# A cached-attention decode step on one core: wo in 16-row chunks, head sums replicated over partitions, half of the wo product as quadrant partial sums

## The chip, the cores and the metric

One core of one Trainium2 chip runs the whole program. The metric is the device time of one execution in microseconds (us), the median of several.

## The reference

One decode step for two sequences. A layer norm of `x` feeds two branches: attention over a cache of 32,768 positions (32 query heads over 8 key/value heads of 128), and a small MLP branch whose result gates the attention output.

```python
x  = A_x                                   # [2, 1, 512] bf16
xn = layernorm(x)
q  = (xn @ wq) as 32 heads of 128          # wq [512, 4096]
s  = softmax(q k^T / sqrt(128)) v @ wo     # k, v: [2, 8, 32768, 128]; wo [4096, 512]
g  = silu(B(xn))                           # layernorm, w3, gelu, w4, residual; with one
                                           # position, w1 and w2 meet only zeros
out = x + s * g
```

The bytes decide: K and V are 2 x 134.2 MB, wq 4.2, w3 and w4 3.7, wo 4.2, together 280.5 MB.

## The kernel before

There are 16 groups, one for each sequence and key/value head. For each, K and V (8.4 MB each) stream into SBUF. VectorE (DVE) transposes K, TensorE (PE) forms scores, ScalarE (ACT) takes exponentials, DVE transposes these, and PE multiplies them by V. The sums of group m are finished ("heads") at the start of the next turn of the loop. SyncE (SP) issues all large loads on one queue, each as soon as its buffer is free:

```python
WO_PARTS = [(0, 2, 0, 2048), (2, 4, 0, 2048), (4, 5, 0, 2048), (5, 6, 0, 2048), (6, 7, 0, 2048),
            (7, 8, 0, 1024), (7, 8, 1024, 1536), (7, 8, 1536, 2048)]
# ... wq, w3, w4 and K of group 0 are issued at once
wait(sp, k_h2)                     # the B branch has read w3 and w4, which lie in V's buffer
load_v(0)
for m in range(1, NG):
    sp.wait_ge(p_k, m)             # the first half of K of group m-1 is used up
    load_k(m)
    sp.wait_ge(p_o, m)             # V of group m-1 is used up
    load_v(m)
wos = A_wo.rearrange("(g p r) d -> p g (r d)", p=128, r=NQ)   # NQ = 4: 4 rows of wo = 4 KB
for i, (g0, g1, c0, c1) in enumerate(WO_PARTS):
    d_wo[i].after(sp.dma_start(out=wo3[:, g0:g1, c0:c1], in_=wos[:, g0:g1, c0:c1]), 16)
```

The heads need two rounds between PE and DVE:

```python
def heads(c):                                                  # DVE
    take(dve, s_x)                                             # PE: head_sums
    then(dve.reciprocal(out=rec[:, :], in_=S))                 # [128, 4]
    dve.tensor_mul(out=on[:, :], in0=oT, in1=rec[:, :]).then_inc(s_on, 1)
    take(dve, s_x)                                             # PE: head_rows, 4 matmuls
    then(dve.tensor_mul(out=xm[:, :, :], in0=xp, in1=mask[:, :, :]))
    dve.tensor_reduce(out=oX[:, c], in_=xm[:, :, :], axis=AX.X, op=ALU.add).then_inc(s_r, 1)
# ... PE, at the end: every row of wo times every head row, four column quarters side by side
def product(i):
    # ... wait for piece i, then for each row r of it:
    for n in range(NQ):
        mm = pe.matmul(s_ps[32 * n:32 * n + BW, :], lhsT=oX[:, ...], rhs=wo3[:, g, c:c + QW], ...)
pe.wait_ge(s_r, NG); product(0); head_sums(); product(1); head_rows()
# ... products 2 to 7; those of the last rows wait for the heads of the last group
```

The softmax here doesn't subtract the row's maximum and nothing guards it: scores larger than these inputs give would overflow.

## Time and profile before

| | before |
|---|---|
| time, median of 3 | 655.39 us (655.20 to 655.46) |
| profiled execution | 655.17 us, span 653.8 us |
| moved from HBM | 280.5 MB |
| first data packet begins, last wo packet ends (packet records) | 1.8 us, 650.7 us |

The page gives each engine's busy time and share of the span first, then the DMA queues (packets, megabytes, share of the time of 16 DMA engines).

```profile
PE 403.5 (62%) x2586; PEld 163.9 (25%) x2586; DVE 339.4 (52%) x425; ACT 75.0 (11%) x179; POOL 6.6 (1%) x24
...
q1 hardware_dynamic: 6748, 280.50, 99.3%
```

The windows view gives, for a stretch of time, the busy time of each engine, then the granted PE clock (the share of its full clock that PE was allowed), the DMA share and GB/s:

```profile
60.00:640.00 580.00, 370.25 (x2265) 148.78 (x2262) 307.90 (x365) 63.10 (x152) 0.00 (x0) 0.80 1.00 433
```

No compute engine is near full and the queue is: the span is the DMA stream, plus 1.8 us before it and about 3 us after. The timeline shows how far the engines wait for it. In the middle of the run (columns: start, duration, engine, line, operation; in brackets the idle time before it) it reads:

```profile
299.63 0.33 SPq L208 DMA_DIRECT2D vbuf<-in_A_v_cache_dram  x1
...
303.13 0.17 DVE L508 TENSOR_REDUCE oX<-xm 128x16 f32 x1 [0.24 <-DVEq L46]
312.67 18.14 DVE L488 STREAM_TRANSPOSE T<-kbuf 128x1024 int32<-128x1024 int32 x16 [9.37 <-DVEq L46]
314.06 9.47 PE L552 MATMUL bank<-T,z 128*128 128x512 bf16 x32 [11.49 <-PEq L46]
...
323.69 0.33 SPq L208 DMA_DIRECT2D kbuf<-in_A_k_cache_dram  x1
```

The heads of the last group's sums end at 303.3 us and DVE then waits 9.4 us for the next K. Each later load is issued while earlier ones are still under way, so the queue does not run dry. How long the queue still had work when a load was issued is called that load's lead below. The end is in the chain of waits (start, duration, what; two DVE operations of 0.3 us and the output transfer follow):

```profile
623.93 26.41 DMA kbuf<-in_A_wo_dram
650.35 0.14 issue
650.48 0.53 PE bank L590 x12
651.01 0.01 issue
651.03 0.32 PE bank L590 x4
```

### The profile page before, as it was taken

The numbers are of one execution on the slowest core, as the hardware profiler recorded it, in microseconds if no ns is written. First come the engines' busy times: TensorE is split into PE (matmuls) and PEld (weight loads), VectorE is DVE, ScalarE is ACT, GpSimd is POOL, SyncE is SP. The second block draws the span as 40 slices with busy tenths as digits, with TensorE's granted clock in tenths as the row PEclk, the third lists the DMA queues.
The fourth block names the chain that finished last, engine by engine and source line by source line (L and its number), as shares of the span: only waits on it lengthen the run. The fifth ranks groups of instructions, "written<-read, shape, count | busy, mean of one in ns | idle before, by whom it ended". The sixth has DMA issues, their size and how long they took to land. (4 is left out here: it accounts for less than half of the span.)

```text
span 653.8 us, 6890 instructions
## 1 busy us (share of the span) xinstructions
PE 403.5 (62%) x2586; PEld 163.9 (25%) x2586; DVE 339.4 (52%) x425; ACT 75.0 (11%) x179; POOL 6.6 (1%) x24
## 2 busy tenths in 40 slices
PE   0448295583838658293774829368383946828785
PEld 0123132221313212131231213223131322303332
DVE  3348091653809256290835719174470926538470
ACT  1400102001010200101020010201001020200100
POOL 3000000000000000000000000000000000000000
PEclk9759787786978868698786978778597886959797
DMA  8999999999999999999999999999999999999997
GB/s 368 435 451 445 442 413 433 441 445 429 417 441 445 441 405 449 441 445 405 441 441 445 417 429 441 445 441 405 449 441 445 401 445 441 445 417 423 429 438 296
DMA packets 6765, 280.57 MB, mean 429 GB/s; under 512 B 736, under 2 KB 1000, under 8 KB 2024
## 3 DMA queue, kind: packets, MB, share of 16 engines
q1 hardware_dynamic: 6748, 280.50, 99.3%
q8 instruction: 3, 0.05, 0.0%
q14 instruction: 2, 0.02, 0.0%
q10 hardware_dynamic: 12, 0.01, 0.0%
HBM read 280.50 MB, written 0.00 MB: 429 GB/s over the span
## 5 line engine op out<-in xcount | busy, mean ns | idle before, releaser
L552 PE MATMUL bank<-T,z 128*128 128x512 bf16 x1024 | 282.2, 425 | 163.4 <-PEq L46 158.7
L488 DVE STREAM_TRANSPOSE T<-kbuf 128x1024 int32<-128x1024 int32 x256 | 290.7, 1206 | 124.7 <-DVEq L46 124.7
L552 PEld LDWEIGHTS bank<-T,z 128*128 128x128 bf16 x1024 | 97.8, 103 | 335.0 <-issue 257.4
L570 PE MATMUL bank<-vbuf,pt 128*16 128x512 bf16 x1024 | 74.7, 457 | 1.5 <-PEq L46 1.5
L467 ACT ACTIVATE ep<-bank 128x512 bf16<-128x512 f32 x32 | 19.1, 597 | 439.2 <-ACTq L46 439.2
L503 DVE RECIPROCAL rec<-bank 128x4 f32<-128x4 f32 x17 | 3.1, 182 | 122.2 <-DVEq L46 122.2
L570 PEld LDWEIGHTS bank<-vbuf,pt 128*16 128x16 bf16 x1024 | 28.0, 103 | 40.5 <-issue 23.5
L495 DVE STREAM_TRANSPOSE pt<-ep 128x512 bf16<-128x512 bf16 x32 | 22.1, 690 | 23.4 <-DVEq L46 23.4
L563 PE MATMUL bank<-sm,ones_f 128*128 128x4 f32 x64 | 9.5, 255 | 29.3 <-PEq L46 29.3
L525 PE MATMUL bank<-sel_o,ob 128*128 128x4 f32 x136 | 18.3, 258 | 14.4 <-PEq L46 14.4
L525 PEld LDWEIGHTS bank<-sel_o,ob 128*128 128x128 f32 x136 | 17.3, 199 | 19.0 <-issue 18.9
L471 ACT COPY ob<-bank 128x512 f32<-128x512 f32 x16 | 9.4, 585 | 104.6 <-ACTq L46 104.6
L460 ACT ACT_TABLE_LOAD x16 | 20.5, 1283 | 0.3
L563 PEld LDWEIGHTS bank<-sm,ones_f 128*128 128x128 f32 x64 | 8.6, 195 | 30.2 <-issue 30.2
L533 PE MATMUL bank<-on,sel_r 128*128 128x4 bf16 x68 | 5.6, 165 | 12.8 <-PEq L46 12.6
L460 ACT COPY z<-qr 32x16 bf16 x64 | 12.9, 201 | 0.7
L506 DVE TENSOR_TENSOR xm<-bank,mask 128x16 f32<-128x16 f32 x17 | 3.0, 175 | 11.7 <-DVEq L46 11.7
L295 PE MATMUL bank<-ident,xn_bf 17*128 17x17 bf16 x4 | 0.3, 177 | 13.5 <-POOL x L286 13.5
L520 PE MATMUL bank<-ident 128*1 128x1 bf16 x64 | 8.3, 165 | 0.0
L520 PEld LDWEIGHTS bank<-ident 128*1 128x1 bf16 x64 | 4.0, 81 | 16.1 <-issue 14.2
L533 PEld LDWEIGHTS bank<-on,sel_r 128*128 128x128 bf16 x68 | 3.1, 100 | 13.7 <-issue 13.7
L467 ACT ACTIVATION_READ_ACCUMULATOR ep<-bank 128x1 f32 x32 | 6.4, 199 | 0.2
(71 smaller groups left out, 57.5 us busy)
## 6 DMA issues: line engine op xcount, KB each, us to landing
kbuf<-in_A_k_cache_dram SPq DMA_DIRECT2D x2, 4096.0 KB, 22.8
vbuf<-in_A_v_cache_dram SPq DMA_DIRECT2D x2, 4096.0 KB, 25.6
kbuf<-in_A_wq_dram SPq DMA_DIRECT2D x1, 4096.0 KB, 12.3
vbuf<-in_B_w_dram SPq DMA_DIRECT2D x2, 1792.0 KB, 17.3
kbuf<-in_A_wo_dram SPq DMA_DIRECT2D x2, 1024.0 KB, 33.2
kbuf<-in_A_wo_dram SPq DMA_DIRECT2D x3, 512.0 KB, 35.7
kbuf<-in_A_wo_dram SPq DMA_DIRECT2D x1, 256.0 KB, 26.4
kbuf<-in_A_wo_dram SPq DMA_DIRECT2D x2, 128.0 KB, 15.6
```

Of the source, the lines that this page charges most:

```text
L460: i = act.copy(out=z[32 * j:32 * j + 32, :, :, c:c + rep], in_=qr[32 * j:32 * j + 32, :, :, bass.ds(m * rep, rep)],)
L467: act.activation(out=eps_[i][:, :], in_=sc[i][:, :], func=ACT.Exp, scale=inv_sqrt_dh, accum_out=rss[i][:, :]).then_inc(s_e, 1)
L471: act.copy(out=ob[:, :], in_=o[:, :]).then_inc(s_ob, 1)
L488: dve.transpose(out=Ts[(NR * i + r) % T_BUFS][:, :].rearrange("p (b t k) -> p t b k", b=NB, t=RT), in_=kt[:, r * W:(r + 1) * W].rearrange( ...
L495: dve.transpose(out=pts[h][:, :, :].rearrange("p r (t h) -> p t r h", h=rep), in_=eps_[i][:, :].rearrange("p (t r h) -> p t r h", r=NR, h= ...
L503: then(dve.reciprocal(out=rec[:, :], in_=S))
L520: pe.matmul(mark_ps, lhsT=ident[:, 0:1], rhs=ident[:, 0:1], start=True, stop=True).then_inc(sem, 1)
L525: mm = pe.matmul(oT, lhsT=ob[:, t * Dh:(t + 1) * Dh], rhs=sel_o[:, t, :], start=(t == 0), stop=(t == VT - 1))
L533: mm = pe.matmul(xp[:, r, :], lhsT=sel_r[:, r, :, :].rearrange("p j w -> p (j w)"), rhs=on[:, :], start=True, stop=True,)
L552: mm = pe.matmul(sc[i][:, :], lhsT=z[:, nb, e, zc:zc + 128], rhs=Tb[:, nb, :, e], start=(r == 0 and nb == 0 and e == 0), stop=(r == NR - 1 ...
L563: pe.matmul(S, lhsT=ones_f[:, :], rhs=sms[h][:, :], start=(h == 0), stop=(h == NPART - 1))
L570: mm = pe.matmul(o[32 * j:32 * j + VT * rep, :], lhsT=pts[h][:, r, a * VT * rep:(a + 1) * VT * rep], rhs=vt[:, u * VT:(u + 1) * VT, :].rea ...
```

## The change

The intent: wo is laid out with 16 consecutive rows per partition instead of 4, so that its pieces move in longer runs. The head sums come out replicated over the partitions (by wider selection matrices), and a mask picks each partition's 16 values, which saves the second round between PE and DVE. wo's first half is multiplied early, four rows at a time in the four 32-row quadrants of PE with 512 columns each, and the four partial sums are merged by four fp32 matmuls. Half of group 0's V is issued before the B branch is done, and the B branch's last product no longer uses the quadrants.

```diff
-WO_PARTS = [(0, 2, 0, 2048), (2, 4, 0, 2048), (4, 5, 0, 2048), (5, 6, 0, 2048), ... ]
+WO_PARTS = [(0, 0, 8), (0, 8, 16), (1, 0, 8), (1, 8, 12), (1, 12, 14), (1, 14, 15), (1, 15, 16)]
-    wos = A_wo.rearrange("(g p r) d -> p g (r d)", p=128, r=NQ)
+    wos = A_wo.rearrange("(g p r) d -> p g (r d)", p=128, r=RS)          # RS = 16
 # SP
     load_k(0)
+    load_half(A_v_cache, vbuf[:, :], s_v, 0, 1)
 ...
-    load_v(0)
+    load_half(A_v_cache, vbuf[:, :], s_v, 0, 0)
 # B branch: h2 in one row block, 14 matmuls in turn instead of four side by side
-            h2_ps[32 * j:32 * j + 32, :], lhsT=h_bf[:, f, :], rhs=w4v[:, f, :],
-            start=(f < NQ), stop=(f >= FK - NQ), tile_position=(0, 32 * j),
+        i = pe.matmul(h2[0:32, :], lhsT=h_bf[:, f, :], rhs=w4v[:, f, :], start=(f == 0), stop=(f == FK - 1))
 # heads on DVE
-        then(dve.reciprocal(out=rec[:, :], in_=S))
-        dve.tensor_mul(out=on[:, :], in0=oT, in1=rec[:, :]).then_inc(s_on, 1)
-        take(dve, s_x)
-        then(dve.tensor_mul(out=xm[:, :, :], in0=xp, in1=mask[:, :, :]))
+        then(dve.reciprocal(out=rec[p0:, :], in_=S[p0:, :]))
+        then(dve.scalar_tensor_tensor(out=xm[p0:, :, :], in0=oT ..., scalar=rec[p0:, 0:1], in1=mask ..., mult, mult))
 # PE, the sums: the selection matrix is the stationary side, 128 columns move
-                oT, lhsT=ob[:, t * Dh:(t + 1) * Dh], rhs=sel_o[:, t, :], ...
+                oT, lhsT=sel_o[:, t, :, :, :] ..., rhs=ob[:, t * Dh:(t + 1) * Dh], ...
-    def head_rows(): ...
 # PE, the end
+    def early(i): ...   # row r into e_ps[32 * (r % 4): ...], 512 columns
+    early(0)
     head_sums()
+    k_e = P(early(1))
+    wait(act, k_e)
+    k_es = A(act.copy(out=e_sb[:, :], in_=e_ps[:, :]))
+    pe.wait_ge(s_r, NG + 2)
+    product(2)
+    wait(pe, k_es)
+    for n in range(NQ):  # merge
+        pe.matmul(s_ps[32 * n:32 * n + BW, :], lhsT=sel_w[:, 0:BW], rhs=e_sb[:, n * QW:(n + 1) * QW], ...)
+    for i in range(3, len(WO_PARTS)):
         mm = product(i)
```

(Cut: buffers, masks, their set-up on POOL and DVE, and the copies that gather the heads' rows.)

More of the change, by code (lines that the diff above doesn't have):

```diff
@@ L21 @@
 EPS = 1e-5
-WO_PARTS = [(0, 2, 0, 2048), (2, 4, 0, 2048), (4, 5, 0, 2048), (5, 6, 0, 2048), (6, 7, 0, 2048), (7, 8, 0, 1024), (7, 8, 1024, 1536), (7, 8, 1536, 2048)]
+WO_PARTS = [(0, 0, 8), (0, 8, 16), (1, 0, 8), (1, 8, 12), (1, 12, 14), (1, 14, 15), (1, 15, 16)]
 class Count:
@@ L87 @@
     NQB = Hkv // NQ
+    NS = Hkv // NQ
+    RS = NQ * NQ
+    WL = Dh // RS
     BS = 16
@@ L106 @@
     rss = [sbuf([128, 1], F32, f"rs{i}") for i in range(NPART)]
-    sms = [sbuf([128, rep], F32, f"sm{i}") for i in range(NPART)]
+    sms = [sbuf([128, NQ * rep * WL], F32, f"sm{i}") for i in range(NPART)]
     z = sbuf([128, NB, 2, ZC], BF16, "z")
     ob = sbuf([128, VT * Dh], F32, "ob")
-    rec = sbuf([128, rep], F32, "rec")
-    on = sbuf([128, rep], BF16, "on")
-    xm = sbuf([128, NQ, rep], F32, "xm")
-    oX = sbuf([128, (NG + 1) * NQ], BF16, "oX")
+    rec = sbuf([128, 1], F32, "rec")
+    xm = sbuf([128, WL, RS], F32, "xm")
+    oA = sbuf([128, (NG + 1) * RS], BF16, "oA")
+    oX = sbuf([128, B * NS * RS], BF16, "oX")
     ident = sbuf([128, 128], BF16, "ident")
@@ L116 @@
     sel_w = sbuf([128, 32], F32, "sel_w")
-    sel_o = sbuf([128, VT, rep], F32, "sel_o")
-    sel_h = sbuf([128, rep], F32, "sel_h")
-    sel_r = sbuf([128, NQ, 4, 32], BF16, "sel_r")
-    mask = sbuf([128, NQ, rep], F32, "mask")
+    sel_t = sbuf([128, VT, rep], F32, "sel_t")
+    sel_o = sbuf([128, VT, NQ, rep, WL], F32, "sel_o")
+    sel_u = sbuf([128, rep], F32, "sel_u")
+    sel_h = sbuf([128, NQ, rep, WL], F32, "sel_h")
+    mask = sbuf([128, WL], F32, "mask")
     x_bf = sbuf([128, D], BF16, "x_bf")
-    xf = sbuf([128, D], F32, "xf")
-    xn = sbuf([128, D], F32, "xn")
-    ln2 = sbuf([128, D], F32, "ln2")
+    xf, xn, ln2 = (Ts[0].bitcast(F32)[:, 0:D], Ts[0].bitcast(F32)[:, D:2 * D], Ts[1].bitcast(F32)[:, 0:D])
     xn_bf = sbuf([128, D], BF16, "xn_bf")
@@ L130 @@
     qT = sbuf([128, 32, NQB * 16], F32, "qT")
+    h4 = sbuf([128, QW], F32, "h4")
     qr = sbuf([128, NB, 2, B * Hq], BF16, "qr")
@@ L147 @@
     sc = banks[0:2]
-    o, S_b, oT_b, xp_b, treg_b, s_b = banks[2:8]
-    S = S_b[:, 0:rep]
-    oT = oT_b[:, 0:rep]
-    xp = xp_b[:, 0:NQ * rep].rearrange("p (r h) -> p r h", h=rep)
+    o, S_b, oT_b, h_ps, treg_b, s_b = banks[2:8]
+    S = S_b[:, 0:1]
+    oT = oT_b[:, 0:Dh]
     treg = treg_b[:, 0:2 * DK * 16].bitcast(BF16)
-    h_ps, h2_ps = xp_b, o
+    h2, e_ps = o, sc[0]
+    e_sb = Ts[2].bitcast(F32)[:, 0:D]
     mark_ps = treg_b[0:1, 0:1]
-    h2 = oT_b[:, 0:QW]
     s_ps = s_b[:, 0:QW]
@@ L197 @@
     w34 = vbuf[:, 0:SLOT]
-    wo3 = kbuf[:, 0:Hq * D].rearrange("p (g c) -> p g c", g=Hkv)
+    wo3 = kbuf[:, 0:Hq * D].rearrange("p (g c) -> p g c", g=NS)
     k_w3 = d_w3.after(sp.dma_start(out=w34[:, 0:W4O], in_=B_w3.rearrange("(p k) f -> p (k f)", k=DK)), 16)
@@ L203, with load_half @@
     )
+    def load_half(cache, dst, sems, m, c):
+        w = slice(c * SLOT, (c + 1) * SLOT)
+        sp.dma_start(out=dst[:, w], in_=row_view(cache, *groups[m])[:, w]).then_inc(sems[c], 16)
     def load(cache, dst, sems, m):
-        src = row_view(cache, *groups[m])
         if m < last:
-            sp.dma_start(out=dst, in_=src).then_inc(sems[0], 16)
+            sp.dma_start(out=dst, in_=row_view(cache, *groups[m])).then_inc(sems[0], 16)
             sp.sem_inc(sems[1], 16)
@@ L211, in load @@
             for c in range(NPART):
-                w = slice(c * SLOT, (c + 1) * SLOT)
-                sp.dma_start(out=dst[:, w], in_=src[:, w]).then_inc(sems[c], 16)
+                load_half(cache, dst, sems, m, c)
     def load_k(m):
@@ L246, with wide @@
     k_z0 = G(pool.memset(z[:, :, :, :], 0.0))
+    def wide(t, n):
+        return t.unsqueeze(1).unsqueeze(3).to_broadcast([128, NQ, rep, n])
     V(dve.memset(s_ps, 0.0))
+    V(dve.memset(o[:, :], 0.0))
     V(dve.memset(S, 1.0))
+    V(dve.memset(oX[:, :], 0.0))
     V(dve.memset(h_bf[:, :, :], 0.0))
@@ L299 @@
         dve.tensor_reduce(
-            out=sel_o[:, :, :],
+            out=sel_t[:, :, :],
             in_=ident[:, :].rearrange("p (j a t h) -> p a t h j", j=4, t=VT, h=rep)[:, 0, :, :, :],
@@ L306 @@
         dve.tensor_reduce(
-            out=sel_h[:, :], in_=ident[:, :].rearrange("p (r h) -> p h r", h=rep), axis=AX.X, op=ALU.add
-        )
-    )
-    V(
-        dve.tensor_copy(
-            out=sel_r[:, :, :, :],
-            in_=ident[:, :].rearrange("p (w r) -> p r w", r=NQ).unsqueeze(2).to_broadcast([128, NQ, 4, 32]),
+            out=sel_u[:, :], in_=ident[:, :].rearrange("p (r h) -> p h r", h=rep), axis=AX.X, op=ALU.add
         )
@@ L317 @@
         dve.tensor_reduce(
-            out=mask[:, :, :],
-            in_=ident[:, :].rearrange("p (h w) -> p h w", h=rep).unsqueeze(1).to_broadcast([128, NQ, rep, 32]),
-            axis=AX.X, op=ALU.add,
+            out=mask[:, :], in_=ident[:, :].rearrange("p (j w) -> p w j", w=WL), axis=AX.X, op=ALU.add
         )
@@ L323 @@
     wait(dve, k_w0)
-    k_mask = V(
+    V(
         dve.tensor_reduce(
             out=sel_w[:, 0:BW:BS],
-            in_=ident[:, :].rearrange("p (j r) -> p r j", j=4)[:, 0:B, :], axis=AX.X, op=ALU.add,
+            in_=ident[:, :].rearrange("p (j r) -> p r j", j=4)[:, 0:BW:BS, :], axis=AX.X, op=ALU.add,
         )
@@ L333 @@
     )
+    wait(pool, k_sh, (g_, g_.n))
+    G(pool.tensor_copy(out=sel_h[:, :, :, :], in_=wide(sel_u[:, :], WL)))
+    for t in range(VT):
+        wait(pool, (g_, g_.n))
+        G(pool.tensor_copy(out=sel_o[:, t, :, :, :], in_=wide(sel_t[:, t, :], WL)))
     wq3 = wq_t[:, 0:DK * HD].rearrange("p (k f) -> p k f", k=DK)
@@ L370 @@
     wait(act, k_qT)
-    wait(pool, k_qT)
+    wait(pool, k_qT, (g_, g_.n))
     for n in range(NQ):
@@ L416 @@
     wait(dve, k)
-    k_hb = V(dve.tensor_mul(out=h_bf[:, :, 0:B], in0=hf, in1=th[:, :, :]))
+    k_hb = V(dve.tensor_mul(out=h_bf[:, :, 0:BW:BS], in0=hf, in1=th[:, :, :]))
     wait(pe, k_hb, k_w4)
     for f in range(FK):
-        j = f % NQ
-        i = pe.matmul(
-            h2_ps[32 * j:32 * j + 32, :], lhsT=h_bf[:, f, :], rhs=w4v[:, f, :],
-            start=(f < NQ), stop=(f >= FK - NQ), tile_position=(0, 32 * j),
-        )
+        i = pe.matmul(h2[0:32, :], lhsT=h_bf[:, f, :], rhs=w4v[:, f, :], start=(f == 0), stop=(f == FK - 1))
     k_h2 = P(i)
-    wait(dve, k_h2)
-    k = V(dve.tensor_copy(out=ln2[:, :], in_=h2_ps[:, :]))
-    wait(pe, k, k_mask)
+    wait(act, k_h2)
     for n in range(NQ):
-        i = pe.matmul(
-            h2[32 * n:32 * n + 32, :], lhsT=sel_w[:, :], rhs=ln2[:, n * QW:(n + 1) * QW],
-            start=True, stop=True, tile_position=(0, 32 * n),
-        )
-    k_h4 = P(i)
+        k_h4 = A(act.copy(out=h4[32 * n:32 * n + 32, :], in_=h2[0:32, n * QW:(n + 1) * QW]))
     wait(dve, k_x4, k_h4)
-    k_tf = V(dve.tensor_add(out=t_f[0:QP, :], in0=xn4[0:QP, :], in1=h2[0:QP, :]))
+    k_tf = V(dve.tensor_add(out=t_f[0:QP, :], in0=xn4[0:QP, :], in1=h4[0:QP, :]))
     wait(act, k_tf)
@@ L449 @@
         load_v(m)
-    wos = A_wo.rearrange("(g p r) d -> p g (r d)", p=128, r=NQ)
-    for i, (g0, g1, c0, c1) in enumerate(WO_PARTS):
-        d_wo[i].after(sp.dma_start(out=wo3[:, g0:g1, c0:c1], in_=wos[:, g0:g1, c0:c1]), 16)
+    wos = A_wo.rearrange("(g p r) d -> p g (r d)", p=128, r=RS)
+    for i, (g, r0, r1) in enumerate(WO_PARTS):
+        w = slice(r0 * D, r1 * D)
+        d_wo[i].after(sp.dma_start(out=wo3[:, g, w], in_=wos[:, g, w]), 16)
     wait(act, k_z0, k_qa, k_qg)
@@ L478, in then @@
         take(dve, s_d)
+    sel = sel_h[:, :, :, :].rearrange("p j h w -> p (j h w)")
     def group(odd):
@@ L494, in group @@
             take(dve, s_e)
+            if i == 0:
+                dve.tensor_scalar_mul(out=sms[0][:, :], in0=sel, scalar1=rss[0][:, 0:1]).then_inc(s_d, 1)
             dve.transpose(
@@ L498, in group, with heads @@
             )
-            dve.tensor_scalar_mul(out=sms[h][:, :], in0=sel_h[:, :], scalar1=rss[i][:, 0:1]).then_inc(s_p, 1)
-    def heads(c):
-        take(dve, s_x)
-        then(dve.reciprocal(out=rec[:, :], in_=S))
-        dve.tensor_mul(out=on[:, :], in0=oT, in1=rec[:, :]).then_inc(s_on, 1)
-        take(dve, s_x)
-        then(dve.tensor_mul(out=xm[:, :, :], in0=xp, in1=mask[:, :, :]))
-        with nc.allow_low_precision(reason="three of the four terms are zero, the fourth is bf16"):
-            dve.tensor_reduce(out=oX[:, c], in_=xm[:, :, :], axis=AX.X, op=ALU.add).then_inc(s_r, 1)
+            if i == 1:
+                take(dve, s_d)
+                dve.scalar_tensor_tensor(
+                    out=sms[1][:, :], in0=sel, scalar=rss[1][:, 0:1], in1=sms[0][:, :], op0=ALU.mult, op1=ALU.add
+                ).then_inc(s_p, 1)
+    def heads(dst, p0):
+        take(dve, s_x)
+        then(dve.reciprocal(out=rec[p0:, :], in_=S[p0:, :]))
+        then(
+            dve.scalar_tensor_tensor(
+                out=xm[p0:, :, :], in0=oT[p0:, :].rearrange("p (w r) -> p w r", w=WL), scalar=rec[p0:, 0:1],
+                in1=mask[p0:, :].unsqueeze(2).to_broadcast([128 - p0, WL, RS]), op0=ALU.mult, op1=ALU.mult,
+            )
+        )
+        with nc.allow_low_precision(reason="all terms but one are zero"):
+            dve.tensor_reduce(
+                out=dst, in_=xm[p0:, :, :].rearrange("p w r -> p r w"), axis=AX.X, op=ALU.add
+            ).then_inc(s_r, 1)
     wait(dve, (v_, v_.n))
@@ L513 @@
         for odd in range(2):
-            heads(bass.ds(t * (2 * NQ) + odd * NQ, NQ))
+            heads(oA[:, bass.ds(t * (2 * RS) + odd * RS, RS)], 0)
             group(odd)
-    heads(slice(NG * NQ, (NG + 1) * NQ))
+    oA4 = oA[:, RS:].rearrange("p (b s j r) -> p j (b s) r", b=B, s=NS, j=NQ)
+    oX4 = oX[:, :].rearrange("p (s r) -> p s r", r=RS)
+    for j in range(NQ):
+        n = B * NS if j < NQ - 1 else B * NS - 1
+        w = slice(32 * j, 32 * j + 32)
+        i_c = dve.tensor_copy(out=oX4[w, 0:n, :], in_=oA4[w, j, 0:n, :])
+    i_c.then_inc(s_r, 1)
+    heads(oX4[32 * (NQ - 1):, B * NS - 1, :], 32 * (NQ - 1))
     def mark(sem):
@@ L525, in head_sums @@
             mm = pe.matmul(
-                oT, lhsT=ob[:, t * Dh:(t + 1) * Dh], rhs=sel_o[:, t, :], start=(t == 0), stop=(t == VT - 1)
-            )
-        mm.then_inc(s_x, 1)
-    def head_rows():
-        take(pe, s_on)
-        for r in range(NQ):
-            mm = pe.matmul(
-                xp[:, r, :], lhsT=sel_r[:, r, :, :].rearrange("p j w -> p (j w)"), rhs=on[:, :],
-                start=True, stop=True,
+                oT, lhsT=sel_o[:, t, :, :, :].rearrange("p j h w -> p (j h w)"),
+                rhs=ob[:, t * Dh:(t + 1) * Dh], start=(t == 0), stop=(t == VT - 1),
             )
@@ L541 @@
         head_sums()
-        head_rows()
         take(pe, s_z)
@@ L560 @@
                 mark(p_k)
-        take(pe, s_p, NPART)
-        for h in range(NPART):
-            pe.matmul(S, lhsT=ones_f[:, :], rhs=sms[h][:, :], start=(h == 0), stop=(h == NPART - 1))
+        take(pe, s_p)
+        pe.matmul(S, lhsT=sms[1][:, :], rhs=ones_f[:, 0:1], start=True, stop=True)
         for h in range(NPART):
@@ L578, with o_rows, early @@
         mark(p_o)
-    BO = Hkv * NQ
+    step = NS * RS // BS
+    oXs = oX[:, :].rearrange("p (i s) -> p i s", s=step)
+    def o_rows(g, r):
+        a = g * RS + r
+        return oXs[:, a // step:a // step + BW, a % step]
+    def early(i):
+        g, r0, r1 = WO_PARTS[i]
+        wait(pe, (d_wo[i], 16))
+        for r in range(r0, r1):
+            j = r % NQ
+            mm = pe.matmul(
+                e_ps[32 * j:32 * j + BW, :], lhsT=o_rows(g, r), rhs=wo3[:, g, r * D:(r + 1) * D],
+                start=(r < NQ), stop=(r >= RS - NQ), tile_position=(0, 32 * j),
+            )
+        return mm
     def product(i):
-        g0, g1, c0, c1 = WO_PARTS[i]
+        g, r0, r1 = WO_PARTS[i]
         wait(pe, (d_wo[i], 16))
-        for g in range(g0, g1):
-            for r in range(c0 // D, c1 // D):
-                for n in range(NQ):
-                    c, a = r * D + n * QW, (g + 1) * NQ + r
-                    mm = pe.matmul(
-                        s_ps[32 * n:32 * n + BW, :], lhsT=oX[:, a:a + BO + 1:BO // BS], rhs=wo3[:, g, c:c + QW],
-                        start=(g == 0 and r == 0), stop=(g == Hkv - 1 and r == NQ - 1),
-                        tile_position=(0, 32 * n),
-                    )
-        return mm
-    pe.wait_ge(s_r, NG)
-    product(0)
+        for r in range(r0, r1):
+            for n in range(NQ):
+                c = r * D + n * QW
+                mm = pe.matmul(
+                    s_ps[32 * n:32 * n + BW, :], lhsT=o_rows(g, r), rhs=wo3[:, g, c:c + QW],
+                    start=(r == 0), stop=(r == RS - 1), tile_position=(0, 32 * n),
+                )
+        return mm
+    pe.wait_ge(s_r, NG + 1)
+    early(0)
     head_sums()
-    product(1)
-    head_rows()
-    for i in range(2, len(WO_PARTS)):
-        if WO_PARTS[i][1] == Hkv and WO_PARTS[i - 1][1] < Hkv:
-            pe.wait_ge(s_r, NG + 1)
+    k_e = P(early(1))
[4 more added lines that the diff above has]
+    wait(pe, k_es)
+    for n in range(NQ):
+        pe.matmul(
+            s_ps[32 * n:32 * n + BW, :], lhsT=sel_w[:, 0:BW], rhs=e_sb[:, n * QW:(n + 1) * QW],
+            start=False, stop=False, tile_position=(0, 32 * n),
+        )
+    for i in range(3, len(WO_PARTS)):
         mm = product(i)
```

## The prediction

> **What bounds the kernel now.** The DMA stream. On the page, queue 1 is busy 99.3% of 16 engines' span (653.8 us), moving 280.5 MB; PE is busy 62%, DVE 52%. In the windows view 60 to 640 us runs at 433 GB/s, DMA share 1.00. The trace's packet records agree: a 65,536-byte packet takes 2,418 ns, times 16 engines 433.6 GB/s. The Trainium skill, "DMA: Bandwidth & Descriptors", section "Where 436 GB/s comes from", gives a ceiling of 435.2 GB/s; this trace stands at it. The stream starts about 1.8 us into the span and ends near 650.7; then matmuls, two DVE operations (0.3 us each) and the output transfer follow (chain of waits). Only these two ends, some 5 us, are not streaming, and the bytes do not change.
>
> **The group loop has slack.** In the timeline of one group DVE idles 9.4 us and PE 11.5 us before the next K arrives at 312.7 us; when V's load is issued (299.6) and K's (323.7), the queue still has 13 and 8 us of work. The change removes four PE matmuls, a DVE round trip (about 1 us) and one fp32 sum matmul pair per group; it adds 128-wide fp32 DVE operations (about 0.3 us, like the 113x128 ones, instead of 0.17 to 0.19). All falls in idle stretches: worth 0 us. So does the prologue: the B branch's last product loses its four-quadrant packing (14 matmuls, about 6 us instead of 1.9 at the low clock) and POOL gets five copies, but K of group 0 only lands at 42.3 us; the engines are ready near 36 now, near 40 after.
>
> **What is on the path.**
> - wo packets. Before: 4 KB 159 ns each, 2 KB 84, 1 KB 46, which fits 8.5 ns a packet plus bytes at the streaming rate. Per engine: 56x159 + 8x84 + 16x46 = 10.31 us. After, 3 MB go in 8 KB packets, an estimate of 310 ns each: 24x310 + 8x159 + 8x84 + 16x46 = 10.12 us. Gain 0.2 us.
> - PE's tail. The last pieces keep their sizes, so the same four matmuls (0.32 us) follow the last landing. But all 64 second-half matmuls and the fp32 merge must wait for the last group's heads (about 647.5) and wo's third MB (about 648.3). At the granted clock of 0.5 seen there, 16 matmuls of 128 columns take 0.61 us; 32 + merge (0.3) + 16 + 8 + 4 + 4 take about 2.8 us, ending near 651.1 to 651.4, against 651.35 now: 0 to +0.3 us.
> - Chance: a few DMA engines finish about 1 us after the rest (650.6 against 649.3) and set the last landing; instruction fetches share these engines and the program changes: plus or minus 0.4 us.
>
> **Predicted time: 655.2 us, 654.5 to 655.9 (8 in 10).** Faster by over 2%: 0.005; within 2%: 0.985; slower by over 2%: 0.01.
>
> **What would show each step.** DMA: queue 1 still at 99% or more, 433 GB/s between 60 and 640 us, 8 KB packets near 310 ns. Loop: longer idle of DVE and PE before K, equal spacing of the K and V issues. Prologue: PE's 14 matmuls stretched, K of group 0 read at the same time. Tail: the last wo piece lands about 0.2 us earlier; the chain still ends in wo's DMA, then PE. PE products back to back from 648.4 us without a DMA wait would show PE's tail as the limit.
>
> **What would make it wrong.** A queue that runs dry, in group 0 or because a later release uses up its 8 us of slack. Heads of the last group later than about 648.5: each us shows one for one. A straggling DMA engine that comes or goes.

## The result

| | before | changed |
|---|---|---|
| time, median of 6 | 655.25 us (655.15 to 655.46) | 655.00 us (654.88 to 655.52) |
| ratio to before, 95% interval | | 0.9997 (0.9984 to 1.0010) |
| packets of queue 1 | 6748 | 6492 |
| PE busy, DVE busy | 403.5, 339.4 us | 390.2, 345.7 us |

A ratio is the mean time of one kernel's fast runs over that of the other's of the same rounds, so not quite the ratio of the medians. The interval contains 1, and in time it reaches from 1.0 us faster to 0.7 us slower: these runs alone show no gain. The profiled execution of the changed kernel happened to be the longest of its six (655.52 us, span 654.2), that of before was near its shortest (655.17 us), so the two spans compare the wrong way round; a later profile of the same changed kernel, quoted in the experiments, has 655.22 us and a span of 653.9.

The same parts of the page and of the windows view, changed kernel:

```profile
PE 390.2 (60%) x2406; PEld 156.8 (24%) x2438; DVE 345.7 (53%) x412; ACT 76.6 (12%) x184; POOL 7.7 (1%) x29
...
q1 hardware_dynamic: 6492, 280.50, 99.2%
```

```profile
60.00:640.00 580.00, 353.27 (x2138) 141.56 (x2166) 313.31 (x352) 63.12 (x152) 0.00 (x0) 0.81 1.00 433
```

The stream runs at the same 433 GB/s with fewer packets. The timeline of the same group:

```profile
299.89 0.33 SPq L213 DMA_DIRECT2D vbuf<-in_A_v_cache_dram  x1
...
302.86 0.37 DVE L518 TENSOR_REDUCE oA<-xm 128x128 f32 x1 [0.24 <-DVEq L46]
313.33 18.14 DVE L489 STREAM_TRANSPOSE T<-kbuf 128x1024 int32<-128x1024 int32 x16 [10.10 <-DVEq L46]
315.10 8.74 PE L562 MATMUL bank<-T,z 128*128 128x512 bf16 x31 [13.29 <-PEq L46]
...
324.00 0.33 SPq L213 DMA_DIRECT2D kbuf<-in_A_k_cache_dram  x1
```

The work saved in the loop came back as idle time: DVE waits 10.1 us for K instead of 9.4, PE 13.3 instead of 11.5. Over groups 1 to 14 DVE's wait is 7.7 to 9.5 us before (mean 8.5) and 8.2 to 10.1 us after (mean 9.0), so the loop's slack is about 9 us rather than 10. The loads of this group are issued at the same moments within 0.3 us; other issues moved more (this V comes at 301.4 us in the later profile of the changed kernel, K of group 1 at 51.8 instead of 53.7 us), but stayed within the lead. In the prologue, lines of the two timelines side by side, before first:

```profile
28.00 1.89 PE L421 MATMUL bank<-vbuf,h_bf 128*32 128x512 bf16 x14 [5.92 <-DVE h_bf L417]
...
42.45 18.15 DVE L488 STREAM_TRANSPOSE T<-kbuf 128x1024 int32<-128x1024 int32 x16 [6.05 <-DVEq L46]
```

```profile
27.36 5.34 PE L428 MATMUL bank<-vbuf,h_bf 128*32 128x512 bf16 x14 [5.70 <-DVE h_bf L425]
...
41.26 18.14 DVE L489 STREAM_TRANSPOSE T<-kbuf 128x1024 int32<-128x1024 int32 x16 [1.65 <-DVEq L46]
```

The 14 matmuls of the B branch take 5.3 us instead of 1.9, and DVE's wait for K of group 0 shrinks from 6.05 to 1.65 us; it still waits. The chain of waits ends the same way as before:

```profile
614.73 36.74 DMA kbuf<-in_A_wo_dram
651.47 0.04 issue
651.52 0.26 PE bank L614 x4
```

PE again ends four matmuls after wo's last landing. In the packet records the last wo packet ends at 650.70 us before, at 651.19 us in this execution, and at 650.85 us in the later profile of the same kernel. So the end moves by 0.3 us between two executions of one program, more than the change is worth, and neither trace of the changed kernel shows wo landing earlier than before.

The mean durations of wo's packets, from the trace's packet records: 1 KB 46 ns, 2 KB 84, 4 KB 159, 8 KB 309, and 2,418 ns for 64 KB. The prediction's estimate for the new 8 KB packets was 310.

### The profile page after: what moved, and what is told of

Its sections match the earlier page's. It is cut to its first block, busy times and chain, and to the rows that moved or that the text cites. A ratio compares the mean times of both kernels' runs of the same rounds, so it can differ in the third digit from the quotient of the medians.

```text
span 654.2 us, 6541 instructions
## 1 busy us (share of the span) xinstructions
PE 390.2 (60%) x2406; PEld 156.8 (24%) x2438; DVE 345.7 (53%) x412; ACT 76.6 (12%) x184; POOL 7.7 (1%) x29
## 3 DMA queue, kind: packets, MB, share of 16 engines
q1 hardware_dynamic: 6492, 280.50, 99.2%
## 5 line engine op out<-in xcount | busy, mean ns | idle before, releaser
L562 PE MATMUL bank<-T,z 128*128 128x512 bf16 x992 | 271.6, 418 | 187.2 <-PEq L46 181.7
L562 PEld LDWEIGHTS bank<-T,z 128*128 128x128 bf16 x1024 | 96.0, 103 | 350.2 <-issue 274.4
L510 DVE RECIPROCAL rec<-bank 128x1 f32<-128x1 f32 (+1 forms) x17 | 2.9, 169 | 122.7 <-DVEq L46 122.7
L544 PE MATMUL bank<-ob,sel_o 128*128 128x128 f32 x136 | 20.6, 298 | 16.4 <-PEq L46 16.4
L572 PE MATMUL bank<-ones_f,sm 128*128 128x1 f32 x32 | 6.6, 277 | 31.3 <-PEq L46 31.3
L544 PEld LDWEIGHTS bank<-ob,sel_o 128*128 128x128 f32 x136 | 17.7, 204 | 21.8 <-issue 21.8
L572 PEld LDWEIGHTS bank<-ones_f,sm 128*128 128x128 f32 x32 | 5.8, 225 | 32.2 <-issue 32.2
L428 PE MATMUL bank<-vbuf,h_bf 128*32 128x512 bf16 x14 | 5.3, 565 | 5.7 <-DVE h_bf L425 5.7
L518 DVE TENSOR_REDUCE oA<-xm 128x128 f32 x16 | 5.9, 366 | 3.8 <-DVEq L46 3.8
L512 DVE SCALAR_TENSOR_TENSOR xm<-bank,rec,mask 128x128 f32<-128x128 f32 (+1 forms) x17 | 6.0, 351 | 2.5 <-DVEq L46 0.2
```

The source lines that it names most:

```text
L512: dve.scalar_tensor_tensor(out=xm[p0:, :, :], in0=oT[p0:, :].rearrange("p (w r) -> p w r", w=WL), scalar=rec[p0:, 0:1], in1=mask[p0:, :].u ...
L518: dve.tensor_reduce(out=dst, in_=xm[p0:, :, :].rearrange("p w r -> p r w"), axis=AX.X, op=ALU.add).then_inc(s_r, 1)
L544: mm = pe.matmul(oT, lhsT=sel_o[:, t, :, :, :].rearrange("p j h w -> p (j h w)"), rhs=ob[:, t * Dh:(t + 1) * Dh], start=(t == 0), stop=(t ...
L562: mm = pe.matmul(sc[i][:, :], lhsT=z[:, nb, e, zc:zc + 128], rhs=Tb[:, nb, :, e], start=(r == 0 and nb == 0 and e == 0), stop=(r == NR - 1 ...
L572: pe.matmul(S, lhsT=sms[1][:, :], rhs=ones_f[:, 0:1], start=True, stop=True)
```

## Experiments

The theory: the time is the length of a DMA stream that never pauses, plus fixed ends. Only wo's packets shorten it; everything on the engines falls into idle time, and PE's tail just keeps up. The rivals: the quarter of a microsecond is noise; or gains in the loop exist and are lost in the tail; or the early V makes up for a slower prologue. Differences from the changed kernel are taken within the same rounds where it ran, otherwise through the kernel before of those rounds, with the changed one 0.15 us under it.

### The changed kernel again: after_again

No edit.

> The changed kernel unaltered, as the reference point of this chip. My theory (a DMA stream that never pauses; only wo's packets count): 0.2 us under the kernel before, that is 655.0 to 655.1 where before is 655.25, ratio about 0.9997. Rival (the 0.25 us seen so far is noise between runs): a median between 0.1 below and 0.1 above before.

655.22 us (655.07 to 655.57) against 655.37 of before (nine runs, 655.07 to 655.53), ratio 0.9999 (0.9986 to 1.0013). The median is 0.15 us lower, as in sign and size expected, but the ranges overlap. These runs alone cannot tell a gain of 0.15 us from none, so the next ones magnify the cause.

### wo in smaller packets: packets_1k and packets_512

```diff
-        d_wo[i].after(sp.dma_start(out=wo3[:, g, w], in_=wos[:, g, w]), 16)
+        dst = wo3[:, g, w].rearrange("p (a b d) -> p b a d", b=2, d=D)   # even rows, odd rows
+        src = wos[:, g, w].rearrange("p (a b d) -> p b a d", b=2, d=D)
+        for e in range(2):
+            d_wo[i].after(sp.dma_start(out=dst[:, e], in_=src[:, e]), 16)
```

(Pieces of one row are left as they are. packets_512 splits all pieces into left and right column halves instead.)

> The changed kernel with wo moved in 1 KB packets: each piece in two transfers, even and odd rows, so that no two rows are contiguous. Same bytes, same pieces, same PE work. My theory: 256 packets of 46 ns per engine are 11.8 us against 10.1 us, and five more completion packets of 9 ns, so 1.7 us slower than the changed kernel (1.4 to 2.0). Rival (the time at the end is set by heads, matmuls or a fixed latency, not by packets): under 0.4 us.

656.08 us (656.02 to 656.37): 0.86 us over the changed kernel of the same rounds, clear of noise but half of the 1.7 expected. The windows view tells why; packets_1k first, then the changed kernel:

```profile
642.00:648.00 6.00, 5.70 (x53) 2.42 (x45) 0.53 (x2) 0.83 (x2) 0.00 (x0) 0.64 1.09 384
```

```profile
642.00:648.00 6.00, 4.98 (x49) 2.21 (x41) 0.90 (x3) 1.17 (x2) 0.00 (x0) 0.72 1.00 420
```

A DMA share of 1.09 cannot be busy time alone: recorded packets overlap. In the packet records, the next packet of an engine usually starts 3 to 4 ns before the recorded end of the one before, at every size. A 1 KB packet therefore occupies 42.3 ns, not 46, and the cost of a packet over pure streaming is 4.7 ns, not 8.5:

| wo, per DMA engine | from durations | from start to start |
|---|---|---|
| before: 56 of 4 KB, 8 of 2 KB, 16 of 1 KB | 10.31 us | 10.02 us |
| changed: 24 of 8 KB, 8 of 4 KB, 8 of 2 KB, 16 of 1 KB | 10.10 us | 9.89 us |
| packets_1k: 256 of 1 KB | 11.78 us | 10.83 us |

Start to start, packets_1k should cost 0.94 us more than the changed kernel; it cost 0.86. The change itself is then worth 0.12 us on the stream, not 0.2: it saves 24 packets per DMA engine, and 24 x 4.7 ns are 0.11 us. The second run was to confirm this:

> The changed kernel with wo moved in 512-byte packets: each piece in two transfers, left and right column halves. In the traces so far the next packet of an engine starts about 3.7 ns before the recorded end of the one before, so a 1 KB packet occupies 42.3 ns and not 46. New theory (packets overlap by 3.7 ns, which leaves 4.7 ns a packet above the streaming rate): 23.5 ns each, 12.05 us against 9.89 us per engine for all of wo, 2.0 to 2.4 us slower than the changed kernel. Old theory (8.5 ns a packet, as predicted): 27.3 ns each, 13.98 against 10.12 us, 3.7 to 4.1 us slower.

658.10 us (657.68 to 658.34), 3.0 us over the changed kernel: between the two ranges, so by its time alone it decides nothing. The trace decides both terms. Its 8,192 packets follow each other at 23 to 24 ns (most recorded as 27), as the new theory said, which gives 2.2 us. The rest is a new wait:

```profile
642.00:644.00 2.00, 2.00 (x29) 0.79 (x21) 0.00 (x0) 0.00 (x0) 0.00 (x0) 0.66 1.01 268
644.00:646.00 2.00, 1.62 (x15) 0.60 (x11) 0.00 (x0) 0.59 (x1) 0.00 (x0) 0.50 0.82 225
646.00:648.00 2.00, 1.43 (x16) 0.85 (x15) 0.63 (x3) 0.00 (x0) 0.00 (x0) 0.99 1.14 343
```

Between 642 and 646 us the stream falls under the 343 GB/s that such packets reach afterwards: 0.39 MB are missing, about 1.1 us at that rate. SP is at the wo issues until 651.4 us in this run (612 to 623 us in the changed kernel), and the chain of waits goes back from wo's last landing to such an issue: fourteen transfers of many small packets were issued too late to keep the queue full. That is an estimate from the windows, and it and the 2.2 us add to slightly more than the 3.0 measured; the profiled execution itself (657.68 us) was only 2.5 us over, so how much of the wait reaches the end is not settled.

### Fewer bytes: quarter_k and half_k

```diff
+        if m == 5 and cache is A_k_cache:
+            w = slice(SLOT // 2, 2 * SLOT)                     # half_k: slice(SLOT, 2 * SLOT)
+            sp.dma_start(out=dst[:, w], in_=row_view(cache, *groups[m])[:, w]).then_inc(sems[0], 16)
+            sp.sem_inc(sems[1], 16)
```

Both are wrong in the part that is not loaded; the comparison with the reference still passed its tolerance.

> The changed kernel with half of one K load (group 5, 4.19 MB) left out; the group works on what the buffer holds, so the result is wrong on purpose. All engine work stays. My theory (the span is the DMA stream): 4,194,304 bytes at 433.6 GB/s are 9.7 us less, 9.4 to 9.9. Rival (engine chains share in the bound): clearly less than that, under 7 us.

646.96 us against 655.29 of before: 8.2 us under the changed kernel instead of 9.7. The missing part is in the trace. SP's timeline, half_k first, then the changed kernel:

```profile
207.66 0.33 SPq L214 DMA_DIRECT2D kbuf<-in_A_k_cache_dram  x1
223.90 0.33 SPq L217 DMA_DIRECT2D vbuf<-in_A_v_cache_dram  x1
```

```profile
207.94 0.33 SPq L213 DMA_DIRECT2D kbuf<-in_A_k_cache_dram  x1
224.34 0.33 SPq L213 DMA_DIRECT2D vbuf<-in_A_v_cache_dram  x1
```

The short K is moved by 223.7 us, just when V is issued, and the packet records show the queue empty or nearly so for 1.34 us from then. 9.67 - 1.34 is 8.33 us. In the profiled execution (647.70 us, the longest of four, 7.4 us under) the gap cost more: the first 64 KB packets after it took 2.6 to 3.4 us on most DMA engines instead of 2.42, 0.6 us more per engine. So the agreement of 8.33 with the median of 8.2 is in part luck. The gap also measures V's lead in this group: 9.67 - 1.34 is 8.3 us from the issue, start-up of the transfer taken off. The prediction had read 13 us, from the issue to DVE's start on K, and in another group.

> The changed kernel with a quarter of group 5's K load (2,097,152 bytes) left out, wrong result on purpose. Leaving out half emptied the queue for 1.3 us, as V's issue had no lead left. My theory: with a quarter the lead lasts, no gap, and the whole of 2,097,152 bytes at 434 GB/s is saved, 4.8 us (4.5 to 5.1). Rival (engines share in the bound, so only 84% of the bytes' time comes back as with the half): 4.0 us.

650.38 us (650.29 to 650.43) against 655.28: 4.75 us under the changed kernel, and no gap. At 434 GB/s the 2,097,152 bytes are 4.83 us. As long as the lead lasts, the whole time of the bytes comes back. This is the strongest evidence that the span is the stream.

### PE's tail: no_quadrant and all_late

```diff
-    early(0)
+    product(0)
     head_sums()
-    k_e = P(early(1)) ... act.copy(e_sb <- e_ps)
+    product(1)
     pe.wait_ge(s_r, NG + 2)
     product(2)
-    # merge: four fp32 matmuls
```

(all_late has product(0) and product(1) after the wait as well.)

> The changed kernel without quadrant partial sums: the first half of wo is multiplied like the second (64 matmuls of 128 columns straight into the final sum), at the same place ahead of the last heads; no merge. My theory (PE waits for wo's pieces at the end anyway): within 0.1 us of the changed kernel. Rival (the partial sums, with their merge and ScalarE copy in the tail, cost or save time at the end): 0.3 us or more either way.

655.22 us (654.95 to 655.29), the median of the changed kernel of the same rounds. The partial sums are worth nothing here: PE waits for wo's pieces either way.

> The changed kernel with the whole wo product (128 matmuls of 128 columns, no partial sums) after the last heads. Heads are ready at about 648.1 us; 128 matmuls at 38 ns (clock 0.5) end near 653.0 instead of 651.8, or at 19 ns (clock 1.0) near 650.6, which is before wo's last piece. My theory: PE's tail becomes the limit, 0.5 to 1.4 us slower than the changed kernel. Rival (wo's landing alone sets the end): within 0.2 us.

656.08 us (655.59 to 656.56): 0.9 us over the changed kernel. The chain of waits no longer ends in the DMA:

```profile
647.79 0.37 DVE oX L518
648.17 0.04 issue
648.21 3.62 PE bank L614 x128
651.83 0.02 issue
651.86 0.30 DVE sg L630
```

128 matmuls back to back follow the last heads, at a granted clock of 0.50 in the windows from 648 to 652 us. They took 28 ns each, not the 38 estimated: that had been read from short series whose start-up was counted in. The Trainium skill, "TensorE: Matmul & The Clock Gate", section "Wait — 56ns, not 53.3ns?", gives 106.7 ns from start to start for 128 columns in the cold state; if four matmuls run at a time, one in each quadrant, that makes 27 ns each by estimate, and this trace's 28 ns agree. So doing part of the product ahead of the last heads matters by about a microsecond, and the kernel before did that already.

### Early V: late_v

```diff
-    load_half(A_v_cache, vbuf[:, :], s_v, 0, 1)      # right after load_k(0)
 ...
-    load_half(A_v_cache, vbuf[:, :], s_v, 0, 0)
+    load_v(0)                                        # after the B branch
```

> The changed kernel with both halves of group 0's V issued after the B branch, as before the change. The B branch's last product ends at 32.7 us and K of group 0 lands at about 41 us, so the queue still has 8 us of work when V is issued. My theory: within 0.1 us of the changed kernel. Rival (the early issue is what made up for the slower B branch): 1 us or more slower.

655.11 us (655.02 to 655.16), against 655.22 of the changed kernel: no difference. Issued at 32.9 us, V of group 0 still found K in the queue.

### More work on DVE: slow_8, slow_14, mid_9, even_6

```diff
             heads(oA[:, bass.ds(t * (2 * RS) + odd * RS, RS)], 0)
+            for _ in range(12):                          # slow_14: 21
+                then(dve.memset(idle_f[:, :], 0.0))
             group(odd)
```

> The changed kernel with twelve needless memsets chained on VectorE in each group after the heads, an estimate of 8 us in all per group (130 us of the whole run). DVE idles about 10 us there. My theory: 0 to 0.2 us slower. Rival (engine work counts in proportion, or disturbs the DMA writes): 1 us or more slower.

665.37 us, 10.2 us slower: a plain miss. Two things were wrong. The chained memsets take 0.77 us each in the trace, 9.2 us a group and not 8. And slack had been read in one group in the middle of the run only: its mean is 9.0 us, and in group 0 DVE has 1.65 us of it (above), so K of group 1 is issued late. slow_8 first, then the changed kernel:

```profile
61.20 0.33 SPq L214 DMA_DIRECT2D kbuf<-in_A_k_cache_dram  x1
```

```profile
51.76 0.33 SPq L213 DMA_DIRECT2D kbuf<-in_A_k_cache_dram  x1
```

The windows of those 5 us, in the same order:

```profile
57.00:62.00 5.00, 5.00 (x24) 2.02 (x23) 5.00 (x5) 0.80 (x2) 0.00 (x0) 1.00 0.40 170
```

```profile
57.00:62.00 5.00, 3.51 (x15) 1.04 (x13) 3.62 (x6) 0.69 (x2) 0.00 (x0) 1.00 1.17 501
```

By the packet records the queue is empty or nearly so for 2.95 us, so the lead of K in group 0 was 9.4 - 2.95, about 6.5 us. Afterwards the engines cannot catch up: DVE waits 0.37 us before K in every group, and it starts on a new K every 38.1 to 39.9 us, 38.7 on average, as long as the stream needs for a group (38.7). So the engines stay behind to the end: there DVE reads the last K from 630.9 us instead of 614.0, wo has landed by 658.4, and PE ends at 662.6, with DVE and PE alone in the chain of waits. In this run also 526 of the 64 KB packets took longer than 2,425 ns (86 in the changed kernel's later profile), 3.3 us per DMA engine in all.

> The same with 21 memsets, about 14 us per group. One group's chain of dependences, from K's landing to the end of its heads, is 28.7 us and K's come every 38.7 us, so 14 us overrun the 10 us of slack by about 4 us. My theory: the DMA queue's own lead (8 us for K) is used up in the first two or three groups, then each group costs about 4 us: 40 to 75 us slower. Rival (engines and DMA overlap freely; DVE would be busy for 36 of 38.7 us): under 5 us.

778.08 us, 123 us slower, in the direction of the theory but more than its range. The 21 memsets took 16.1 us a group, not 14, and the slack is 9.0 us, not 10: each group overran by about 7 us instead of 4, as DVE's starts on K show, 45.8 us apart on average against 38.7; and the packet records show 15 gaps of 5.5 to 9.1 us between 59 and 710 us, about 100 us of idle time per DMA engine. Once a group's chain is longer than the stream's 38.7 us, the engines set the pace.

(The loop is written three times, for groups 0 and 1, 2 to 13, and 14 and 15; only the middle one has the memsets.)

> The changed kernel with twelve chained memsets (9.2 us by the trace of the earlier run) on VectorE after the heads of groups 2 to 13 only, twelve of sixteen groups, 111 us in all. Theory: the loop has 10 us of slack per group, and the earlier run's 10 us came from group 0 (1.65 us of slack, DMA gap of 3 us) and from the tail alone: 0 to 0.3 us slower than the changed kernel. Rival (added engine work disturbs the stream everywhere): 3 us or more slower.

656.23 us (656.03 to 656.25), 1.1 us slower: above the range of 0 to 0.3, far from the rival's 3. The stream kept its rate and its queue never ran empty (the window, then DVE's start on K of group 7):

```profile
60.00:640.00 580.00, 358.30 (x2167) 142.04 (x2165) 383.08 (x495) 63.12 (x152) 0.00 (x0) 0.81 1.00 433
...
315.00 15.95 DVE L490 STREAM_TRANSPOSE T<-kbuf 128x1024 int32<-128x1024 int32 x14 [0.37 <-DVEq L46]
```

The memsets took up all of the slack: DVE waits 0.37 us instead of 10.10 here, and as little in all of groups 2 to 13; its starts on K are 38.7 us apart on average, just the stream's pace. So 111 us of DVE's time (70 busy, the rest pauses between chained memsets) cost 1.1 us. The last wo packet ends 1.0 us later than in the changed kernel's later profile. 182 long packets (against 86) make up 0.3 us per engine of that; the longer program also fetched four blocks of 8 KB instructions instead of two on the DMA engines. Which of these makes the rest is not shown.

```diff
+            if odd == 0:
+                then(dve.tensor_reduce(out=idle_f[:, :], in_=<ident repeated to 128x48x128>, axis=AX.X, op=ALU.add))
```

> The changed kernel with one needless VectorE reduction of 6,144 elements per partition after the heads of every second group (groups 0, 2 to 14; not the last), an estimate of 6.5 us each from the 0.67 us of the 512-element reduction's rate less its fixed part, some 52 us in all. It adds two instructions to the loop, not a tripled loop like the run before. Theory (engine work inside the slack is free; the 1.1 us of that run came with its longer program or its larger delay): 0 to 0.2 us slower than the changed kernel. Rival (added engine work costs the stream 1% of itself, as 1.1 of 111 us): 0.5 us slower. If the reduction turns out much longer than 7 us, group 0 loses its lead and a gap in the DMA queue near 59 us shows it.

656.50 us, but spread from 655.06 to 657.27: inconclusive. Each reduction took 6.54 us as estimated. The fastest run equals the changed kernel, and the profiled one (655.49 us) has no gap in its queue. But in group 0 K was issued at 57.2 us, 5.4 us late, close to the whole lead of 6.5, so gaps in some of the unprofiled runs are possible; no trace shows one.

## Why the prediction was right, point by point

- **Bound.** Right. The queue is busy 99.2% with 433 GB/s, and leaving out 2.1 MB took out 4.75 us of the 4.83 they need.
- **The loop is worth 0 us.** Right for what the change does: DVE's and PE's waits before K grew and the issues stayed in place. It should not be read as "any work up to 10 us is free": the mean slack is 9.0 us, adding 9.2 us to twelve groups used it up and cost 1.1 us, and adding it to all cost 10.
- **Prologue.** Right: 5.3 us for the B branch, and K of group 0 still had to be waited for. DVE started on it at 41.3 us, not at 42.5 as before and as forecast; it did so in late_v too, so the early V is not the cause, which stays open. The early V did nothing for the time (late_v).
- **wo packets, 0.2 us.** Right in mechanism, too large. The step that added packet durations was off, since recorded packets overlap by about 4 ns: the term is 0.12 us by the starts, supported by packets_1k (0.94 expected from starts, 0.86 measured). The gain of the change itself, 0.15 to 0.25 us by medians, lies within noise, so it is consistent with 0.12 us but not shown by times alone. The forecast sign of it, wo landing 0.2 us earlier, was not seen: 651.19 and 650.85 us against 650.70.
- **PE's tail, 0 to +0.3 us.** Right: four matmuls end it as before, and undoing the quadrant sums changes nothing. The 38 ns a matmul were too slow an estimate; it is 28 in a long series.
- **Leads of 13 and 8 us.** Too large where the runs measure them: counted until the queue is really empty, 8.3 us (V of group 5) and 6.5 us (K of group 1). Only part of the difference is an error of reading. The groups differ: in the trace before, DVE starts on K 13.0 us after V's issue in group 7, but 11.4 us after it in group 5. The rest is that DVE starts some 2 us after the queue has moved on, and that a transfer needs about 1.2 us to start.
- **Chance of 0.4 us from a straggling DMA engine.** The last wo packet ended at 650.85 and 651.19 us in two executions of the changed kernel, so the term was of the right size. It is also larger than all that the change is worth.

The total fell well inside the range: 655.0 against 655.2 predicted. That alone says little: the range of 1.4 us would have held the unchanged 655.25 us too. What the runs support is the step that nearly all of the change is worth nothing.

## What to carry to other kernels

When one DMA queue streams all the time, cost a change by bytes, packets and the two ends, and give engine work inside the loop no value unless it moves an issue past the queue's lead. Measure that lead by experiment, and in the first groups too, where it was the smaller of the two measured here. For a term of a tenth of a per cent, magnify its cause until it stands clear of noise, as with the small packets here.

## What the Trainium skill lacked or had wrong

- "DMA: Bandwidth & Descriptors", section "Why small descriptors are slow (HBM only)", gives about 3 cycles of fixed cost a packet, and 32 bytes of descriptor metadata for each operation. With the page's 32-byte beats and the 850 MHz that it states elsewhere, the estimate is three cycles and one more for the 32 bytes, 4.7 ns. Start to start, the runs show 4.1 to 4.7 ns above a sixteenth of the 435.2 GB/s, from 512 bytes to 64 KB (4.7 from 2 KB up), so the page agrees with them. What no page says is that a trace's packet durations overlap by 3 to 4 ns, so that their sum (DMA share 1.09 with 1 KB packets) overstates the time.
- The same page, section "Where 436 GB/s comes from", says without a condition that for transfers from HBM to SBUF the HBM side, about 358 GB/s, binds. Its own table of measurements just above has 425 GB/s for a single core, and names 358 as each core's share when both cores of a pair stream. This single core streamed at 433 GB/s for 580 us, 0.5% under the page's 435.2, so here 358 did not bind.
- No page tells how far ahead a load must be issued to keep such a queue full. For the start-up alone, the same page's "Specifications" give a first-byte latency of about 0.6 us, and the runs agree: the first packet on an empty queue begins 0.63 and 0.64 us after the end of the 0.33 us issue (half_k: 224.23 and 224.86 us; slow_8: 61.53 and 62.17 us). Until most DMA engines move data it is 1.2 us from the start of the issue.
- No page says that packets take longer right after a queue has been empty: there the first 64 KB packet of a DMA engine mostly took 2.6 to 3.4 us instead of 2.42 (half_k, slow_8). Packets of over 2,425 ns also appear without a gap, 10 of them in quarter_k and 182 in mid_9. The cause is not shown.
